# A fused attention kernel: instruction orders planned with TensorE's tile-mode turns counted once per turn, and jobs cut into single matmuls

## The chip, the core and the metric

One core of a Trainium2 chip runs the whole program in one launch. The metric is device time in microseconds, the median of several executions. Lower is better. The engines are TensorE (PE; its weight loads are PEld), VectorE (DVE), ScalarE (ACT), GpSimd (POOL) and SyncE (SP, which issues DMAs).

## The reference

Two attention blocks with their own inputs run side by side, each on 2,048 tokens of width 512 with 32 heads of 16. Their outputs are joined along the last axis.

```python
B, S, D = 1, 2048, 512
H = 32; Dh = D // H
# block A: linear attention
phi = lambda t: jnp.where(t > 0, t + 1, jnp.exp(t)) + 1e-6
pq, pk = phi(q), phi(k)
kv = jnp.einsum("bhsd,bhse->bhde", pk, v)
z = jnp.einsum("bhsd->bhd", pk)
num = jnp.einsum("bhqd,bhde->bhqe", pq, kv)
den = jnp.einsum("bhqd,bhd->bhq", pq, z)[..., None] + 1e-6
a = heads_joined(num / den) @ wo
# block B: softmax attention
scores = jnp.einsum("bhqd,bhkd->bhqk", q, k) * Dh ** -0.5
b = heads_joined(einsum("bhqk,bhkd->bhqd", softmax(scores), v)) @ wo
```

In both, q, k and v come from `x @ wqkv`. Most of the work is block B's exponential: 32 heads x 2,048 x 2,048 scores.

## The kernel before, in words

**Blocks.** The scores of block B are cut into 2,048 blocks of 128 keys by 512 queries, each for one head. They lie in 32 units. A unit is one group of eight heads (`Gp`, four of them), one stretch of 512 queries (`c`, four) and the even or odd heads of the group (`e_`, two), so a unit has 64 blocks: 16 stretches of keys for 4 heads. A score matmul (L709) contracts over 32 rows only, so that four of them, one for each 32-row quarter of TensorE's array, run side by side. It writes one block into one of seven PSUM banks.

**Two ways from scores to probabilities.** ScalarE takes two or three neighbouring banks in one exponential (L903, 1024 or 1536 columns wide). The banks of these pairs and triples are 0 and 1 with 2, and 4 and 5 with 3 (`SLOT`, `OPT`), used in turn. VectorE takes single blocks, or two at once where their banks are neighbours (L805), from the banks 6, 3 and 2 (`DSET`): it computes the bits of an approximate exponential as whole numbers. GpSimd makes two shifted copies of each such block with an integer addition (L977, mostly two blocks at once). The three versions are weighted by three scaled copies of v (L556) and summed, which makes the approximation finer. So a block of ScalarE costs one value matmul, and a block of VectorE costs three.

**Values.** A value matmul (L1031) has 17 output columns (16 of v and the sum) and sits in one quarter of the array's columns. Four of them, one for each head of the unit, run side by side: a round. They accumulate in one PSUM bank, `pPV`. At the end of a unit VectorE transposes that bank (L1051), takes reciprocals and normalizes (L1058, L1059).

**Jobs.** Projections, the linear block A and the output projections are cut into jobs: some matmuls into one of the banks of `DSET`, then VectorE or ScalarE work, and sometimes DMAs. L472, L547, L578, L604, L657 and others are their matmuls. Block A's phi needs 32 exponentials of 512 columns on ScalarE (L569).

**The planner.** The order on each engine is not written by hand. While the program is built, a list scheduler in Python (the loop at the end of the kernel function) keeps a planned clock `T` for each engine and a planned duration for each step. It repeatedly picks the step that can start first. What it can pick for TensorE: `fill_act_cand`, a pair or triple of scores for ScalarE, with up to two blocks for VectorE behind it (`d_pick`, `d_emit`); `fill_d_cand`, blocks for VectorE alone; `pv_cand`, a batch of value matmuls of up to `PVR` rounds; `job_cand`, the first matmuls of a job; and later pieces of jobs that run (`halves` cuts their matmuls into `parts`). Near the moment at which ScalarE would run out of scores (`dry`), only steps that end in time for the next pair may be picked. Planned idle time on TensorE of over about 0.2 us is filled with dummy matmuls on a zero weight (`fill_in`, L1237), which stand in the program as any other instruction. The result is one fixed order for each engine, with semaphores between them.

**Planned durations before.** A score group counts 0.33 us, a batch of values 0.1 + 0.215 for each round, a job matmul of 512 columns 0.26. TensorE works in three arrangements of its array: four quarters of rows for scores, four quarters of columns for values and dummies, the whole array for jobs. What a turn between them costs is contained in these numbers, whatever stands before a step.

Of the kernel before, what the change touches and what calls it, by code (L numbers as in the profile page):

```python
# [233 lines left out]
def bass_concat_heads__linear_attn_block__softmax_full_mha__prompt_kernel(nc, A_x, A_wqkv, A_wo, B_x, B_wqkv, B_wo, out):  # L234
# [3 lines left out]
    NGP = 4  # L238
# [19 lines left out]
    DLOW = 1.0  # L258
# [13 lines left out]
    with es:  # L272
# [132 lines left out]
        LAT = 0.12  # L405
        T = {"pe": 0.0, "act": 0.0, "dve": 0.0, "pool": 0.0, "dma": 0.0}
# [10 lines left out]
        class Job:  # L417
# [11 lines left out]
            def stage_done(self, i, end, bk, bi):  # L429
                if i == self.rel and bi is not None:  # L430
                    bfree[bi] = end + LAT
                    held[bi] = False
                for st, tk in self.gives:
                    if st == i:
                        tok[tk] = end + LAT
                if i + 1 < len(self.stages):
                    eng, dur, fn = self.stages[i + 1]
                    lat = LAT if eng != "pe" or eng != self.stages[i][0] else 0.0
                    push(eng, end + lat, JPR if eng == "pe" else (0 if i + 1 <= self.rel and self.bank else min(self.prio, 2)), dur,
                         lambda st_, en_, fn=fn: (fn(bk), self.stage_done(i + 1, en_, bk, bi)))  # L440
# [10 lines left out]
        MM = 0.26  # L451
# [50 lines left out]
        def gram_x(t4, **kw):  # L502
            def f(e, bk, i):
                tl, cc = divmod(i, 4)
                t = 4 * t4 + tl
                return e.matmul(f32v(bk)[:, tl * 128:(tl + 1) * 128], lhsT=xTb[:, cc, t * 128:(t + 1) * 128], rhs=xTb[:, cc, t * 128:(t + 1) * 128],
                                start=(cc == 0), stop=(cc == 3))
            return Job(halves(f, [("xTb", t) for t in range(4 * t4, 4 * t4 + 4)], n=16, parts=4, dur=0.07) + [
                        ("dve", 0.6, f_ev("dve", lambda e, bk: e.tensor_reduce(GRX[:, t4:t4 + 1], f32v(bk), axis=AX.X, op=ALU.max), [], [("GRX", t4)]))],
                       [("xTb", t) for t in range(4 * t4, 4 * t4 + 4)], [(4, ("GRX", t4))], **kw)  # L510

        def gram_w(kind, **kw):
            def f(e, bk, i):
                Gp, cc = divmod(i, 4)
                w = Wb[:, cc, kind * 512 + Gp * 128:kind * 512 + Gp * 128 + 128]
                return e.matmul(f32v(bk)[:, Gp * 128:(Gp + 1) * 128], lhsT=w, rhs=w, start=(cc == 0), stop=(cc == 3))
            gw = GRW[:, kind, :].rearrange("p (a h) -> p a h", h=8)
            return Job(halves(f, [("Wb", kind, g) for g in range(NGP)], n=16, parts=4, dur=0.07) + [
                        ("dve", 0.6, f_ev("dve", lambda e, bk: e.tensor_reduce(GRW[:, kind, :], f32v(bk).rearrange("p (h c) -> p h c", c=16), axis=AX.X,
                                                                                op=ALU.add, apply_absolute_value=True), [], [("GRW", kind)])),  # L520
                        ("dve", 0.15, f_op("dve", lambda e: e.tensor_tensor(gw, gw, ZMk[:].unsqueeze(1).broadcast_to([128, 4, 8]), op=ALU.mult),
                                           [("GRW", kind), "ZMk"], [("GRW", kind)])),
                        ("dve", 0.15, f_op("dve", lambda e: e.tensor_reduce(TOP[:, 1 + kind:2 + kind], GRW[:, kind, :], axis=AX.X, op=ALU.max),
                                           [("GRW", kind)], [("TOP", 1 + kind)]))],
                       [], [(6, ("TOP", 1 + kind))], rel=4, **kw)
# [17 lines left out]
        def v4_job(t4, Gp, **kw):  # L543
# [6 lines left out]
            st = halves(mm, [("Wb", 2)] + [("xTb", t) for t in ts], n=16, parts=2, dur=0.085)  # L550
# [24 lines left out]
        def akv_mm(t2, hp, kind):  # L575
            def mm(e, bk, i):
                tt, cc = divmod(i, 4)
                return e.matmul(f32v(bk)[:, 256 * tt:256 * tt + 256], lhsT=xTa[:, cc, (t2 + tt) * 128:(t2 + tt + 1) * 128],  # L578
                                rhs=Wa[:, cc, 512 * kind + 256 * hp:512 * kind + 256 * hp + 256], start=(cc == 0), stop=(cc == 3))
            return halves(mm, ["Wa", ("xTa", t2), ("xTa", t2 + 1)], n=8, parts=2, dur=0.14)  # L580
# [11 lines left out]
        def akvsum_job(hp, bl, **kw):  # L592
# [3 lines left out]
            st = halves(mm, [("KNa", t) for t in range(NT)] + [("VNa", t) for t in range(NT)] + ["VNa1"], n=16, parts=4, dur=0.1)  # L596
# [14 lines left out]
        def aden_job(sc, **kw):  # L611
# [5 lines left out]
            return Job(halves(f, [("PQT", 0, bq) for bq in range(4)] + [("RHZ", bq) for bq in range(4)], n=16, parts=4, dur=0.0625) + [  # L617
# [4 lines left out]
        def anum_job(sc, tl, **kw):  # L622
# [7 lines left out]
            return Job([("pe", 0.36, f_pe(f, [("PQT", 0, bq) for bq in range(4)] + [("RHA", bq) for bq in range(4)])),  # L630
# [206 lines left out]
        def fill_act_cand():  # L837
# [13 lines left out]
            if pt_room(2, start + 0.5) is None:  # L851
# [4 lines left out]
                start = later[0] - 0.5 + 1e-6  # L856
            def run(st, en):
# [37 lines left out]
                if tk:  # L895
                    d_emit(tk, en + 0.05)
                    T["pe"] = en + 0.05
# [12 lines left out]
            return start, 0.33, run  # L910

        def fill_d_cand():
# [15 lines left out]
            return at, 0.32, run  # L928
# [59 lines left out]
        def pv_cand():  # L988
# [13 lines left out]
            def batch(rd):  # L1002
                byg = [[x for x in rd if x[1][2] == g] for g in range(4)]
                best = None
                for rounds in range(1, PVR + 1):
                    bt = sum([q_[:rounds] for q_ in byg], [])
                    n = len(bt)
                    sc_ = n / (0.1 + 0.215 * rounds)
# [15 lines left out]
            dur = 0.1 + 0.215 * bb[1]  # L1024
# [166 lines left out]
        def job_cand():  # L1191
            best = None
            bi = d_bank()
            for lst, pr in ((urgent, 0.5), (early, 2), (bjobs, 2.2), (urgent2, 2.3), (ajobs, 2.5)):
                for pos, j_ in enumerate(lst[:1] if lst is not urgent2 else lst[:8]):
# [3 lines left out]
                    eng, dur, fn = j_.stages[0]  # L1199
# [5 lines left out]
                    if best is None or (st, pr) < (best[0], best[1]):  # L1205
                        def run(st_, en_, j_=j_, lst=lst, fn=fn):
# [6 lines left out]
                            j_.stage_done(0, en_, bk, b_)  # L1213
# [30 lines left out]
        while True:  # L1244
            opts = []
            for eng in T:
# [6 lines left out]
                if best is not None:  # L1253
                    c_ = best[2]
                    opts.append((best[1], c_[1], eng, c_[3], c_[4], c_))
            fa = fill_act_cand()
            if fa is not None:
                opts.append((fa[0], 0, "pe", fa[1], fa[2], None))
            fd = fill_d_cand()
            if fd is not None:  # L1260
                opts.append((fd[0], 3, "pe", fd[1], fd[2], None))
# [3 lines left out]
            if pc is not None:  # L1265
                opts.append((pc[0], pc[3], "pe", pc[1], pc[2], None))
            jc = job_cand()
            if jc is not None:
                opts.append((jc[0], jc[1], jc[2], jc[3], jc[4], None))
# [13 lines left out]
            st, _, eng, dur, run_, c_ = o  # L1283
# [96 lines left out]
```

## Time and profile before

| | |
|---|---|
| median of 3 runs | 740.53 us (740.44 to 741.14) |
| the profiled execution's own time | 741.09 us |
| its span, first to last instruction | 739.4 us |
| ScalarE busy | 711.2 us (96%) |
| TensorE busy by matmul records | 676.5 us (91%) |
| VectorE busy | 516.2 us (70%) |
| GpSimd busy | 327.2 us (44%) |
| blocks by ScalarE and by VectorE | 1,521 and 527 |

The page gives for each engine the time in which at least one of its instructions was running, and their number. A group's row has the line of code, the engine, the operation, what it writes and reads with the shape, the count, then busy time and the mean duration in ns of one, and behind the second bar the idle time of the engine just before, with what ended it. Durations of neighbours on one engine can overlap, so the pace of an engine is read from starts that follow each other. A row of the timeline has the start, the time from the first start to the last end, the engine, the line, the operation, and the count of merged instructions. The clock column says which share of full speed TensorE was granted; 1.00 is full.

### The profile page before, as it was taken

Reading aid. Unit: us, or ns where it says so; the run is one execution under the profiler, and the core shown is the slowest. Engines: PE = TensorE matmul, PEld = TensorE weight load, DVE = VectorE, ACT = ScalarE, POOL = GpSimd, SP = SyncE. Lnnn points to the kernel's source line nnn. Section 1 sums busy time; section 2 is a strip of 40 time slices with the busy share of each in tenths; the row PEclk is TensorE's granted clock in tenths of the full one; section 3 lists DMA queues with packets and bytes.
Section 4 is the critical chain, followed back from the end, with each engine's and each line's share of the span. In section 5 each row is a group of like instructions: output and inputs, shape, how many; then the busy total and the mean of one; then the engine's idle time right before and its main releaser. Section 6 shows DMA issues by size and latency. Waiting matters only on the chain.

```text
span 739.4 us, 15721 instructions
## 1 busy us (share of the span) xinstructions
PE 676.5 (91%) x6483; PEld 226.9 (31%) x6534; DVE 516.2 (70%) x865; ACT 711.2 (96%) x691; POOL 327.2 (44%) x562
## 2 busy tenths in 40 slices
PE   6999999999999999999899999889899999999996
PEld 4322333333333333233222223234222222222222
DVE  3887776765677667733688778845878777867771
ACT  3999999999999999999999999999999999999995
POOL 3455544522454434500356645500645475636560
PEclk9999999999999999999999999999999999999999
DMA  9900000000000000000201000000101100000001
GB/s 222 233 2 1 2 1 9 7 9 8 3 1 1 2 1 8 9 13 4 52 1 29 22 9 12 10 19 22 30 1 29 37 2 30 1 25 6 15 16 33
DMA packets 36573, 17.33 MB, mean 23 GB/s; under 512 B 27536, under 2 KB 35984, under 8 KB 36496
## 3 DMA queue, kind: packets, MB, share of 16 engines
q1 hardware_dynamic: 35408, 15.61, 8.8%
q8 instruction: 53, 0.87, 0.5%
q10 hardware_dynamic: 1088, 0.66, 0.3%
q14 instruction: 24, 0.20, 0.1%
HBM read 4.46 MB, written 4.19 MB: 12 GB/s over the span
## 4 chain that ended last, share of the span: by engine, by line
ACT 88%; PE 8%; issue 2%; DVE 1%; ACTq 0%; POOL 0%; POOLq 0%
ACT PT L903 86%; PE pS L709 3%; PE pPV L1031 2%; ACT EA L569 2%; PE pS L657 1%; PE pS L472 1%; PE pS L1120 0%; PE pS L1078 0%; DVE PT L805 0%; PE pPV L1237 0%; PE pS L1237 0%; ACT KNa L454 0%; PE pS L547 0%; PE pS L1109 0%; DVE KM L486 0%
## 5 line engine op out<-in xcount | busy, mean ns | idle before, releaser
L903 ACT ACTIVATE PT<-pS 128x1024 f16<-128x1024 f32 (+1 forms) x653 | 702.4, 1332 | 9.6 <-PE pS L709 9.4
L977 POOL INT64_ADD PT<-PT x537 | 319.8, 608 | 385.2 <-DVE PT L805 339.0
L805 DVE TENSOR_SCALAR PT<-pS 128x512 int16<-128x512 f32 (+1 forms) x503 | 339.5, 708 | 88.4 <-PE pS L709 84.0
L709 PE MATMUL pS<-QT,KM 32*128 32x512 bf16 x2048 | 281.8, 386 | 37.9 <-ACT PT L903 27.6
L1031 PE MATMUL pPV<-PT,VV 128*17 128x512 f16 x3102 | 269.8, 383 | 0.5 <-DVE OT L1051 0.4
L709 PEld LDWEIGHTS pS<-QT,KM 32*128 32x128 bf16 x2048 | 73.1, 91 | 280.6 <-ACT PT L903 228.7
L1031 PEld LDWEIGHTS pPV<-PT,VV 128*17 128x17 bf16 x3102 | 63.0, 88 | 122.7 <-issue 92.6
L1051 DVE STREAM_TRANSPOSE OT<-pPV 128x512 f32<-128x512 f32 x32 | 22.8, 713 | 30.5 <-PE pPV L1031 30.2
L578 PE MATMUL pS<-Wa,xTa 128*128 128x256 bf16 x256 | 38.7, 275 | 0.8 <-DVE PT L805 0.5
L472 PE MATMUL pS<-xTb,Wb 128*128 128x512 bf16 x98 | 29.8, 383 | 5.2 <-issue 2.1
L454 DVE CAST KNa<-pS 128x512 bf16<-128x512 f32 x30 | 20.5, 686 | 18.5 <-PE pS L657 17.0
L1237 PE MATMUL pPV<-xTb,ZW 128*17 128x256 bf16 x180 | 31.7, 274 | 0.0
L570 DVE TENSOR_SCALAR EA<-EA 128x512 bf16<-128x512 bf16 x32 | 11.7, 365 | 22.5 <-ACT EA L569 22.4
L569 ACT ACTIVATE EA<-pS 128x512 bf16<-128x512 f32 x32 | 26.1, 815 | 0.0
L578 PEld LDWEIGHTS pS<-Wa,xTa 128*128 128x128 bf16 x256 | 19.9, 97 | 17.9 <-issue 9.7
L547 PE MATMUL pS<-Wb,xTb 128*128 128x128 bf16 x256 | 19.5, 220 | 0.5
L1237 PEld LDWEIGHTS pPV<-xTb,ZW 128*17 128x17 bf16 x180 | 14.4, 91 | 15.0 <-issue 10.2
L657 PE MATMUL pS<-WOa,KNa 128*128 128x512 bf16 x52 | 15.6, 381 | 2.6 <-issue 1.4
L604 PE MATMUL pS<-xTa,Wa 128*128 128x512 bf16 x55 | 16.6, 383 | 1.3 <-issue 0.8
L482 DVE CAST QT<-pS 128x512 bf16<-128x512 f32 x15 | 10.3, 688 | 10.0 <-PE pS L472 9.8
L1059 DVE TENSOR_TENSOR OT<-OT,ZR 128x256 bf16<-128x256 f32 x32 | 16.6, 520 | 0.6
L547 PEld LDWEIGHTS pS<-Wb,xTb 128*128 128x128 bf16 x256 | 14.4, 98 | 8.0 <-issue 4.5
(78 smaller groups left out, 223.8 us busy)
## 6 DMA issues: line engine op xcount, KB each, us to landing
out_dram<-KNa SPq DMA_DIRECT2D x30, 128.0 KB, 1.7
Wa<-in_A_wqkv_dram SPq DMA_DIRECT2D x1, 1536.0 KB, 7.9
KM<-KR SPq DMA_DIRECT2D x96, 16.0 KB, 1.8
Wb<-in_B_wqkv_dram SPq DMA_DIRECT2D x2, 384.0 KB, 4.9
Wb<-in_B_wqkv_dram SPq DMA_DIRECT2D x1, 512.0 KB, 4.3
WOb<-in_B_wo_dram SPq DMA_DIRECT2D x1, 512.0 KB, 8.7
WOa<-in_A_wo_dram SPq DMA_DIRECT2D x1, 512.0 KB, 9.5
ON<-in_B_x_dram ACTq DMA_DIRECT2D x1, 256.0 KB, 2.7
```

Source lines behind the costliest of these rows:

```text
L472: return e.matmul(f32v(bk), lhsT=Wb[:, cc, kind * 512 + Gp * 128:kind * 512 + Gp * 128 + 128], rhs=xTb[:, cc, sc * 512:(sc + 1) * 512], st ...
L547: return e.matmul(f32v(bk)[:, tl * 128:(tl + 1) * 128], lhsT=xTb[:, cc, t * 128:(t + 1) * 128], rhs=Wb[:, cc, 1024 + Gp * 128:1024 + Gp * ...
L569: ("act", 0.06 + n * 0.000833, f_ev("act", lambda e, bk: e.activation(EA[:, q, 0:n], f32v(bk)[:, c0:c0 + n], ACTF.Exp), [], [("EA", q)])),
L578: return e.matmul(f32v(bk)[:, 256 * tt:256 * tt + 256], lhsT=xTa[:, cc, (t2 + tt) * 128:(t2 + tt + 1) * 128], rhs=Wa[:, cc, 512 * kind + 2 ...
L657: return e.matmul(f32v(bk), lhsT=src, rhs=WO[:, hb, :], start=(hb == 0), stop=(hb == 3))
L709: return e.matmul(dst, lhsT=KM[32 * g:32 * g + 32, Gp % 2, e_, j * 128:(j + 1) * 128], rhs=QT[32 * g:32 * g + 32, Gp % 2, c * 512:(c + 1) ...
L805: sch.add("dve", lambda e: e.tensor_scalar(PTi[:, i * 512:(i + n) * 512], PS[:, b0 * 512:(b0 + n) * 512], ESC, EB, op0=ALU.mult, op1=ALU.add),
L903: sch.add("act", lambda e: e.activation(PT[:, p0 * 512:p0 * 512 + w], PS[:, use[0] * 512:use[0] * 512 + w], ACTF.Exp, scale=SC), reads=[(" ...
L977: sch.add("pool", lambda e: e.int64_add(PTl[:, pos * 128:pos * 128 + w], PTl[:, p0 * 128:p0 * 128 + w], v_), reads=[("PT", p0 + i) for i i ...
L1031: sch.add("pe", lambda e, g=g, j=j, hl=hl, pi=pi, k=k, first=first, last_=last_: e.matmul(PVb[32 * g:32 * g + 17, 0:512], lhsT=VV[:, Gp % ...
L1051: sch.add("dve", lambda e: e.transpose(OT[:, 0, :], PVb[:, 0:512]), reads=[("PV", g) for g in range(4)], writes=[("OT", 0)])
L1237: ins = e.matmul(dst, lhsT=ZW[:, 0:17], rhs=xTb[:, 0, 0:256], start=first, stop=first, tile_position=(0, 32 * g))
```

## The change

The planner counts a turn of TensorE between scores (mode `q`) and anything else (mode `w`) as 0.1 us (`SW`), once, when the mode of the picked step differs from the one before. The steps themselves become shorter: a score group 0.222, a batch of values 0.2155 for each round + 0.005, a job matmul of 512 columns 0.226, and the narrower ones in proportion.

A job's part is no longer one piece. `halves` cuts each part into pieces of about 0.24 us, so single matmuls of 512 columns, two of 256, or four of 128. `Job.issue` and `Job.ran` hand them to the planner one after the other, and between two pieces it may pick a score group.

Batches of values have at most two rounds (`PVR` 2 instead of 3) and are taken from a lower yield on (`PVQ` 11 instead of 12.5). A new rule in `fill_act_cand` lets a score group wait, as long as ScalarE doesn't run dry, until two banks for VectorE's blocks are free (`WAITN`, `WAITM`), if VectorE has less than `DLOW` of work queued. `TEND`, by which jobs get the time from which they may start, is 670 instead of 640. No instruction of the kernel computes anything else than before; which blocks go to which engine, and the order, come out of the planner anew.

```diff
-    PVR = 3
-    PVQ = 12.5
-    PVO = 16
+    PVR = 2
+    PVQ = 11
+    PVO = 12
     RES = 8
+    WAITN = 2
+    WAITM = 0.05
...
-    TEND = 640.0
+    TEND = 670.0
...
-    DLOW = 1.0
+    DLOW = 1.5
...
+        SW = 0.1
+        mode = ["w"]
...
-        MM = 0.26
+        MM = 0.226
...
             w = n // parts
-            return [("pe", w * dur, mk(i * w, (i + 1) * w)) for i in range(parts)]
+            q = max(1, round(w * dur / 0.24))
+            while w % q:
+                q -= 1
+            v = w // q
+            return [("pe", w * dur, None, [(v * dur, mk(i * w + x * v, i * w + (x + 1) * v)) for x in range(q)]) for i in range(parts)]
...
+            if nfill[0] >= 2 and d_backlog(start) < DLOW and not lagging(start):
+                late = T["act"] + sum(exps) - 0.222 - SW - LAT - WAITM
+                now = sum(bfree[x] is not None and bfree[x] <= start + 0.05 for x in DSET)
+                if now < WAITN:
+                    t1 = sorted(bfree[x] for x in DSET if bfree[x] is not None and start + 0.05 < bfree[x] <= late)
+                    if t1:
+                        start = t1[0]
...
-            return start, 0.33, run
+            return start, 0.222, run
...
-            dur = 0.1 + 0.215 * bb[1]
+            dur = 0.2155 * bb[1] + 0.005
...
-                lim = max(dry - fa[1] - LAT - 0.05, fa[0])
-                keep = [o for o in opts if o[2] != "pe" or o[4] is fa[2] or o[0] + o[3] <= lim or o[0] + 1e-9 < fa[0] - o[3]]
+                lim = max(dry - fa[1] - SW - LAT - 0.05, fa[0])
+                keep = [o for o in opts if o[2] != "pe" or o[4] is fa[2] or o[0] + o[3] + (SW if mode[0] == "q" and o[6] == "w" else 0) <= lim]
...
             if eng == "pe":
                 fill_in(st)
+                if md != mode[0]:
+                    st = max(st, T["pe"] + SW)
+                    mode[0] = md
```

The added lines shift the numbers: L709 becomes L732, L805 L828, L903 L933, L977 L1007, L1031 L1061, L1237 L1268, L578 L601, L472 L495, L547 L570. What the planner makes of it in the program:

| in the built order | before | after |
|---|---|---|
| exponentials of 1024, 1536 and 512 columns (L903, L933) | 436, 216, 1 | 548, 116, 1 |
| VectorE's blocks, single and two at once (L805, L828) | 479, 24 | 497, 53 |
| GpSimd's additions for two blocks and for one (L977, L1007) | 517, 20 | 598, 10 |
| value matmuls (L1031, L1061) | 3,102 | 3,254 |
| rounds that they make | 889 | 944 |
| runs of score matmuls with nothing between | 632 | 666 |
| dummy matmuls (L1237, L1268) | 208 | 238 |

TensorE at the first job of block A, before (L709 scores, L1031 values, L578 the job):

```order
L709 MATMUL pS<-QT,KM 128x512 x4
L1031 MATMUL pPV<-PT,VV 17x512 x12
L709 MATMUL pS<-QT,KM 128x512 x3
L578 MATMUL pS<-Wa,xTa 128x256 x8
L709 MATMUL pS<-QT,KM 128x512 x3
L1031 MATMUL pPV<-PT,VV 17x512 x12
```

and after, at the same job:

```order
L732 MATMUL pS<-QT,KM 128x512 x3
L1061 MATMUL pPV<-PT,VV 17x512 x4
L601 MATMUL pS<-Wa,xTa 128x256 x2
L732 MATMUL pS<-QT,KM 128x512 x3
L601 MATMUL pS<-Wa,xTa 128x256 x4
L732 MATMUL pS<-QT,KM 128x512 x3
L601 MATMUL pS<-Wa,xTa 128x256 x2
L732 MATMUL pS<-QT,KM 128x512 x3
L1061 MATMUL pPV<-PT,VV 17x512 x8
```

The eight matmuls of the job stood in one piece. Now they are in three pieces with a score group between each two, and a batch of values has eight matmuls where it had twelve.

ScalarE from its first exponential on, before:

```order
L903 ACTIVATE PT<-pS 128x1536
L903 ACTIVATE PT<-pS 128x1024 x13
L903 ACTIVATE PT<-pS 128x1536
L903 ACTIVATE PT<-pS 128x1024
L903 ACTIVATE PT<-pS 128x1536
L903 ACTIVATE PT<-pS 128x1024 x3
L903 ACTIVATE PT<-pS 128x1536
```

and after:

```order
L933 ACTIVATE PT<-pS 128x1024 x21
L933 ACTIVATE PT<-pS 128x1536
L933 ACTIVATE PT<-pS 128x1024 x21
L933 ACTIVATE PT<-pS 128x1536 x5
L933 ACTIVATE PT<-pS 128x1024
```

Pairs take the place of triples: the bank that made a pair a triple (2 or 3) goes to a block for VectorE.

VectorE after its first reciprocals, before (L805 the blocks, L482 a job's copy):

```order
L805 TENSOR_SCALAR PT<-pS 128x1024
L805 TENSOR_SCALAR PT<-pS 128x512
L1059 TENSOR_TENSOR OT<-OT,ZR 128x16x16
L805 TENSOR_SCALAR PT<-pS 128x512 x5
L482 CAST QT<-pS 128x512
L805 TENSOR_SCALAR PT<-pS 128x512 x12
```

and after:

```order
L828 TENSOR_SCALAR PT<-pS 128x1024
L828 TENSOR_SCALAR PT<-pS 128x512 x4
L828 TENSOR_SCALAR PT<-pS 128x1024
L828 TENSOR_SCALAR PT<-pS 128x512 x4
L828 TENSOR_SCALAR PT<-pS 128x1024
L828 TENSOR_SCALAR PT<-pS 128x512 x4
```

More of its instructions take two blocks at once.

More of the change, by code (lines that the diff above doesn't have):

```diff
@@ L507, in f @@
                                 start=(cc == 0), stop=(cc == 3))
-            return Job(halves(f, [("xTb", t) for t in range(4 * t4, 4 * t4 + 4)], n=16, parts=4, dur=0.07) + [
+            return Job(halves(f, [("xTb", t) for t in range(4 * t4, 4 * t4 + 4)], n=16, parts=4, dur=0.058) + [
                         ("dve", 0.6, f_ev("dve", lambda e, bk: e.tensor_reduce(GRX[:, t4:t4 + 1], f32v(bk), axis=AX.X, op=ALU.max), [], [("GRX", t4)]))],
@@ L517, in gram_w @@
             gw = GRW[:, kind, :].rearrange("p (a h) -> p a h", h=8)
-            return Job(halves(f, [("Wb", kind, g) for g in range(NGP)], n=16, parts=4, dur=0.07) + [
+            return Job(halves(f, [("Wb", kind, g) for g in range(NGP)], n=16, parts=4, dur=0.058) + [
                         ("dve", 0.6, f_ev("dve", lambda e, bk: e.tensor_reduce(GRW[:, kind, :], f32v(bk).rearrange("p (h c) -> p h c", c=16), axis=AX.X,
```

53 lines of the change are left out of this document (33 added, 20 removed).

## The prediction

> **What bounds the kernel now.** I read the page first, then the chain, then the groups with their shapes kept apart, then the stretch between the first and the last exponential, and last single rows of the timeline, because a mean duration does not say how fast an engine accepts work.
>
> ```profile
> span 739.4 us, 15721 instructions
> PE 676.5 (91%) x6483; PEld 226.9 (31%) x6534; DVE 516.2 (70%) x865; ACT 711.2 (96%) x691; POOL 327.2 (44%) x562
> ...
> ACT 88%; PE 8%; issue 2%; DVE 1%; ACTq 0%; POOL 0%; POOLq 0%
> ACT PT L903 86%; PE pS L709 3%; PE pPV L1031 2%; ACT EA L569 2%; PE pS L657 1%; PE pS L472 1%; PE pS L1120 0%; PE pS L1078 0%; DVE PT L805 0%; PE pPV L1237 0%; PE pS L1237 0%; ACT KNa L454 0%; PE pS L547 0%; PE pS L1109 0%; DVE KM L486 0%
> ```
>
> ScalarE's exponentials (L903) are 86% of the chain. From here I call L709 a score matmul, L1031 a value matmul, L1237 a dummy, and the other TensorE work jobs. A block is one 128x512 score tile. The next row is the stretch from the start of the first exponential to the end of the last (14.69 and 729.53 us).
>
> ```profile
> 14.69:729.53 714.84, 663.80 (x6399) 218.41 (x6448) 509.50 (x847) 707.56 (x685) 321.59 (x544) 1.00 0.08 19
> ```
>
> The columns are PE, PEld, DVE, ACT, POOL, the clock, DMA. ScalarE is busy 707.56 of 714.84 us, so only 7.3 us of idle lie in the stretch. Outside it lie 14.7 us of start and 9.9 us of end. That gives the accounting that I use: 14.7 + 707.6 of ScalarE work + 7.3 idle + 9.9 = 739.5, against a span of 739.4, and 1.7 us around the span make this execution's 741.09. The median of the runs shown is 740.53, so 0.56 is taken off at the end.
>
> The groups show who shares the softmax blocks:
>
> ```profile
> L903 ACT ACTIVATE PT<-pS 128x1024 f16<-128x1024 f32 x436 | 441.8, 1187 | 6.7 <-PE pS L709 6.7
> L903 ACT ACTIVATE PT<-pS 128x1536 f16<-128x1536 f32 x216 | 326.5, 1627 | 2.9 <-PE pS L709 2.8
> L977 POOL INT64_ADD PT<-PT x537 | 319.8, 608 | 385.2 <-DVE PT L805 339.0 <-PE pS L709 34.1 <-issue 6.4
> L805 DVE TENSOR_SCALAR PT<-pS 128x512 int16<-128x512 f32 x479 | 310.9, 682 | 83.2 <-PE pS L709 79.2 <-issue 0.3
> ...
> L805 DVE TENSOR_SCALAR PT<-pS 128x1024 int16<-128x1024 f32 x24 | 29.3, 1220 | 5.2 <-PE pS L709 4.8
> ```
>
> Of the 2,048 blocks, ScalarE takes 436x2 + 216x3 and one more alone = 1,521. VectorE takes 479 + 24x2 = 527. The means of 1187 and 1627 ns are not what one exponential costs, because neighbours overlap. Their price is read from starts that follow each other without a gap:
>
> ```profile
> 67.87 0.89 ACT L569 ACTIVATE EA<-pS 128x512 bf16<-128x512 f32 x1
> 68.35 15.02 ACT L903 ACTIVATE PT<-pS 128x1024 f16<-128x1024 f32 x15
> 83.02 0.84 ACT L569 ACTIVATE EA<-pS 128x512 bf16<-128x512 f32 x1
> ...
> 324.24 0.85 ACT L569 ACTIVATE EA<-pS 128x512 bf16<-128x512 f32 x1
> 324.71 11.12 ACT L903 ACTIVATE PT<-pS 128x1536 f16<-128x1536 f32 x8
> 335.36 0.96 ACT L569 ACTIVATE EA<-pS 128x512 bf16<-128x512 f32 x1
> ```
>
> Eight wide ones take 335.36 - 324.71 = 10.65, or 1.331 us each. The fifteen from 68.35 to 83.02 stand in ScalarE's order as thirteen of 1024 and two of 1536: (14.67 - 2.66) / 13 = 0.924 us. An L569 takes 0.48 (67.87 to 68.35). The check is 436x0.924 + 216x1.331 + 33x0.48 (32 of L569 and the one exponential of 512) = 706.2, against 707.56 busy. So these prices carry the run.
>
> **The change, part by part.** The built order of the changed kernel has 548 exponentials of 1024, 116 of 1536 and one of 512, which is 1,445 blocks. VectorE has 497 + 53x2 = 603. So 76 blocks leave ScalarE. There are 112 more exponentials of 1024 (112x0.924 = 103.5) and 100 fewer of 1536 (133.1), so ScalarE has 29.6 us less to do. A second reading bounds it from above: (707.56 - 33x0.48) / 1,521 = 0.455 per block, times 76, is 34.6. From that goes the fixed part of twelve more instructions: 1.331 - 0.924 = 0.407 per block leaves 0.11 fixed, so 1.3, which makes 33.3. I take 29.6, the value from single rows, and keep 33.3 for the low end.
>
> The moved blocks cost the others. VectorE: 18x0.682 + 29x1.220 = 47.7, so 516 becomes 564 of about 711 us. GpSimd: 598 wide and 10 narrow additions instead of 517 and 20, so at most 81x0.608 = 49, and 327 becomes 376. Both stay well below ScalarE on the whole run. TensorE gets 152 more value matmuls (3,254 for 3,102, two extra for each moved block), more score groups and finer job pieces. Its slots, from the timeline:
>
> ```profile
> 299.70 0.83 PE L1031 MATMUL pPV<-PT,VV 128*17 128x512 f16 x12
> ...
> 300.46 0.40 PE L709 MATMUL pS<-QT,KM 32*128 32x512 bf16 x4
> ...
> 300.78 0.61 PE L1031 MATMUL pPV<-PT,VV 128*17 128x512 f16 x8
> ...
> 301.33 0.39 PE L709 MATMUL pS<-QT,KM 32*128 32x512 bf16 x3
> ```
>
> Twelve value matmuls, three rounds of four side by side, hold TensorE 0.76 us until the next score group, and eight hold it 0.55. So a round is 0.21 and 0.12 is the turn to scores. A score group with the turn away from it is 0.32 (300.46 to 300.78), so a group with both turns is 0.44. Job and dummy slots:
>
> ```profile
> 91.19 0.61 PE L578 MATMUL pS<-Wa,xTa 128*128 128x256 bf16 x4
> ...
> 91.73 0.39 PE L709 MATMUL pS<-QT,KM 32*128 32x512 bf16 x2
> ...
> 726.73 1.04 PE L1237 MATMUL pPV<-xTb,ZW 128*17 128x256 bf16 x8
> ```
>
> Four job matmuls of 256 columns take 0.54 - 0.12 = 0.42, or 0.41 ns a column. Eight dummies take 1.04 with a tail of about 0.27, or 0.11 each. Counted in the two orders: 632 runs of scores before, 666 now; 889 rounds of value matmuls (up to four column tiles each) before, 944 now; 208 dummies before, 238 now; about 297,000 job columns in both. The sum before is 632x0.44 + 889x0.21 + 122 + 208x0.11 = 278 + 187 + 122 + 23 = 610 us. After it is 293 + 198 + 122 + 26 = 639. Against a stretch of 714.84 the margin was 105 us. Against 714.84 - 29.6 = 685 it is 46. That margin hides the 29 us of added TensorE work, and without it they would cost up to 29 us.
>
> The page's own busy time says something else: 663.80 busy, and with 29 more it is 693, over the 685. By that reading TensorE paces the changed kernel. In the Trainium skill, Perfetto Trace Analysis, section Identifying the Most-Contended Engine, matmul busy time is called no good measure of how near TensorE is to its limit. This trace agrees that it is none, though here it reads high (663.8 against 610 of slots). By the rule the sum stays with the slots; by the busy time it would be the second rival's.
>
> The finer pieces bring 34 more score groups, each with a turn to scores and one away. A turn shows as 0.32 for a group that at 0.21 a round should take 0.21, so 0.11 to 0.12. Then 34x2x0.11 = 7.5 us, which stand within the 293. In the Trainium skill, TensorEngine Tiling (Array Packing), section Key Properties, a change of tiling mode is said to drain TensorE, which speaks against more changes. The rows agree that a turn costs, and set its size at 0.11.
>
> What remains is how much ScalarE waits. The waits of before:
>
> ```profile
> ACT PT L903 <- PE pS L709: 9.4, 12, 2.3
> PEld pS L709 <- ACT PT L903: 228.7, 544, 1.2
> ...
>   PEld pS L709: 15.4, 45
>   PEld pS L578: 4.9, 15
>   PEld pS L657: 3.9, 15
>   PEld pS L472: 3.2, 11
>   PEld pPV L1031: 3.1, 12
>   PEld pS L547: 2.0, 7
>   PEld pS L627: 1.3, 5
> ```
>
> The indented rows are those who waited for VectorE's blocks (L805). ScalarE waited for scores only 12 times, 0.78 us each. TensorE waited for a free score bank 544 times, so it mostly runs ahead. With the margin halved I expect about 4 more waits, 3 us. Below, none of the 7.3 is left. Above, the second rival. The new rule that holds a score group back until a second vector bank is free writes no wait of its own into the program. It only decides which score matmuls stand together, and the extra one waits behind the pair that ScalarE needs. Queued behind it on TensorE are value matmuls and then the next pair. Start and end stand alike in both orders, so 14.7 and 9.9 stay.
>
> The sum: 741.09 - 29.6 + 3.0 = 714.5 for an execution like the profiled one, and 714.5 - 0.56 = 713.9 beside the median: 714.
>
> **The rivals.** *The turns reach ScalarE.* If the 34 added groups fall where no margin is left, their 7.5 us come on top of 711.5 - 0.56 with the 3 us of waits: about 721. For it: job pieces of one or two matmuls now stand between pairs. Against it: 544 waits for a free bank. In the Trainium skill, TensorEngine Tiling (Array Packing), Key Properties, the drain at a change of mode is what would act here. Chance 0.10.
>
> *TensorE and VectorE pace together.* The seven rows of waits on VectorE are 33.8 us. Grown with its blocks (603/527) they are 39, and 639 + 39 = 678 of 685: no margin. If a third of the 39 reaches ScalarE, 711.5 + 13 = 724. For it: TensorE's queue is in order, so a vector score that waits holds the pair behind it. Against it: those waits are short, 0.34 us each in the first row (15.4/45). Chance 0.16.
>
> *Slower: scores that wait for a vector bank in front of a pair.* The price is 0.34 us a wait. The margin of 46 has to be used up and then the 29.6, so 76 us, which are about 220 more waits of this kind among 666 groups, every third. With 240 of them it is 746. VectorE at 79% speaks a little for it, the 45 such waits of before against it. Chance 0.03.
>
> *Waits vanish.* If ScalarE's idle of 7.3 goes almost wholly and the 33.3 holds, it is 741.09 - 33.3 - 2 - 0.56 = 705. Chance 0.07.
>
> *It changes nothing.* The blocks move, yet just as much idle appears on ScalarE, 29.6 us or about 38 more waits of 0.78. Chance 0.02.
>
> **How the numbers follow.** My forecast, between 707 and 719, keeps 0.62. All cases but two are faster: 0.95. A measurement of this kernel can tell about 0.2% from no change (1.5 us; its three runs span 740.44 to 741.14). Within that lies 0.02, slower 0.03. The range takes in most of the first two rivals and the low end of the gain: 705 to 728.
>
> **What would show it.** Right: about 1,445 blocks in the L903 successor with ScalarE busy about 678 us and idle between exponentials near 10; TensorE's waits for ScalarE's banks fewer than 544 and shorter in sum; VectorE near 564 busy, GpSimd near 370. Wrong: ScalarE idle before exponentials of 20 us or more, spread over many waits (the turns, if TensorE was running jobs; the second rival, if VectorE released it), or a start or end that grew. If the prices of an exponential differ from 0.924 and 1.331, the first term fails.

## The result, and the profile after

The changed kernel takes 718.81 us (median of 4 runs, 717.50 to 721.31) against 740.83 in the same measurement: a ratio of 0.9707, 95% interval 0.9679 to 0.9735. The forecast was 714, between 705 and 728. The profiled execution is the slowest of the four, 721.31 us with a span of 719.6, and it is the one that is read here. The top of its page and its chain:

```profile
span 719.6 us, 16347 instructions
PE 693.6 (96%) x6716; PEld 227.8 (32%) x6716; DVE 551.8 (77%) x912; ACT 686.8 (95%) x703; POOL 372.2 (52%) x633
...
PE 72%; ACT 21%; DVE 4%; issue 2%; POOL 0%; ACTq 0%; DVEq 0%; POOLq 0%
PE pPV L1061 26%; PE pS L732 24%; ACT PT L933 20%; PE pS L680 4%; PE pS L495 4%; PE pS L601 3%; DVE PT L828 2%; PE pPV L1268 2%; PE pS L570 2%; PE pS L627 2%; ACT EA L592 1%; DVE OT L1081 1%; PE pS L650 1%; PE pS L618 1%; PE pS L529 1%
```

ScalarE was 88% of the chain and is 21%. TensorE, 8% before, is 72%, spread over values, scores and jobs. ScalarE's busy share of 95% shows none of that. Next the groups with shapes apart, then the stretch from the first exponential to the end of the last (columns as before):

```profile
L933 ACT ACTIVATE PT<-pS 128x1024 f16<-128x1024 f32 x548 | 524.3, 1049 | 13.8 <-PE pS L732 10.7 <-DVE PT L828 0.5
L933 ACT ACTIVATE PT<-pS 128x1536 f16<-128x1536 f32 x116 | 167.4, 1491 | 0.5 <-PE pS L732 0.3
```

```profile
13.43:709.65 696.22, 681.80 (x6632) 219.66 (x6630) 545.69 (x895) 683.16 (x697) 367.61 (x617) 0.99 0.08 21
```

The stretch is 696.2 us instead of 714.8. ScalarE is busy 683.2 of it and idle 13.1, where it was busy 707.6 and idle 7.3. The start is 13.4 us (14.7 before) and the end 9.9 as before. The mean duration of an exponential of 1024 fell from 1187 to 1049 ns: they begin less far ahead of the end of the one before (half of all exponentials by 0.28 us or more before the change, by 0.13 after it). The waits between the two engines moved as well:

```profile
PEld pS L732 <- ACT PT L933: 149.0, 376, 1.2
...
PEld pS L732 <- DVE PT L828: 17.9, 47, 2.4
...
ACT PT L933 <- PE pS L732: 11.0, 17, 3.3
```

TensorE waits for a score bank of ScalarE 376 times instead of 544. ScalarE waits for scores 17 times instead of 12, and one wait is 3.3 us long. That one lies in the start, seen engine by engine: GpSimd, VectorE, ScalarE, then TensorE's clock in three stretches.

```profile
L1007 POOLq MODIFY_POOL_CONFIG  x2: 11/11/11, 16.6 to 16.6; - x2
```

```profile
22.86 1.20 POOL L1007 INT64_ADD PT<-PT  x2 [6.37 <-PE pS L732]
```

```profile
20.76 0.74 DVE L509 TENSOR_SCALAR KM<-pS,PAR 128x512 bf16<-128x512 f32 x1
24.16 1.29 DVE L828 TENSOR_SCALAR PT<-pS 128x512 int16<-128x512 f32 x2 [2.65 <-POOL PT L1007]
25.36 1.23 DVE L579 TENSOR_SCALAR VV<-VV 128x544 bf16<-128x544 bf16 x2
```

```profile
27.83 1.02 ACT L933 ACTIVATE PT<-pS 128x1024 f16<-128x1024 f32 x1 [3.30 <-PE pS L732]
29.40 1.02 ACT L933 ACTIVATE PT<-pS 128x1024 f16<-128x1024 f32 x1 [0.54 <-PE pS L732]
```

```profile
20.00:23.40 3.40, 3.38 (x43) 1.48 (x35) 1.50 (x3) 3.40 (x4) 0.55 (x1) 1.00 1.03 177
23.40:25.50 2.10, 0.00 (x0) 0.00 (x0) 1.34 (x3) 1.13 (x2) 2.10 (x5) 1.00 1.09 215
25.50:32.60 7.10, 6.97 (x40) 1.23 (x40) 5.82 (x10) 3.70 (x4) 4.59 (x9) 0.52 1.08 291
```

GpSimd's first addition starts at 22.86 us, 6.3 us behind its change of configuration at 16.6 (before: 23.11). In all fourteen traces of this case, those of the experiments below included, it comes 5.7 to 6.9 us behind the change of configuration, whatever the order asks for. The planner takes GpSimd as free from the start. The new order asks VectorE for more blocks early, and one of them waits 2.65 us for GpSimd. TensorE stands behind VectorE with no matmul from 23.4 to 25.5. Then the granted clock is 0.52 for 7 us, and ScalarE is busy only 3.7 of 7.1 us. In the Trainium skill, GPSIMD Engine Reference, section Instruction dispatch, the first call of a freshly loaded GpSimd kernel is said to cost about 6 us more, with no instruction of its own in the profile. The 6.3 us here agree.

### The profile page after: what moved, and what is told of

It reads as the page before. It is cut to its first block, busy times and chain, and to the rows that moved or that the text cites. A ratio compares the mean times of both kernels' runs of the same rounds, so it can differ in the third digit from the quotient of the medians.

```text
span 719.6 us, 16347 instructions
## 1 busy us (share of the span) xinstructions
PE 693.6 (96%) x6716; PEld 227.8 (32%) x6716; DVE 551.8 (77%) x912; ACT 686.8 (95%) x703; POOL 372.2 (52%) x633
## 4 chain that ended last, share of the span: by engine, by line
PE 72%; ACT 21%; DVE 4%; issue 2%; POOL 0%; ACTq 0%; DVEq 0%; POOLq 0%
PE pPV L1061 26%; PE pS L732 24%; ACT PT L933 20%; PE pS L680 4%; PE pS L495 4%; PE pS L601 3%; DVE PT L828 2%; PE pPV L1268 2%; PE pS L570 2%; PE pS L627 2%; ACT EA L592 1%; DVE OT L1081 1%; PE pS L650 1%; PE pS L618 1%; PE pS L529 1%
## 5 line engine op out<-in xcount | busy, mean ns | idle before, releaser
L933 ACT ACTIVATE PT<-pS 128x1024 f16<-128x1024 f32 (+1 forms) x665 | 672.4, 1126 | 14.3 <-PE pS L732 11.0
L1007 POOL INT64_ADD PT<-PT x608 | 364.8, 613 | 319.8 <-DVE PT L828 276.2
L828 DVE TENSOR_SCALAR PT<-pS 128x512 int16<-128x512 f32 (+1 forms) x550 | 380.8, 733 | 67.7 <-PE pS L732 61.4
L1061 PE MATMUL pPV<-PT,VV 128*17 128x512 f16 x3254 | 290.5, 385 | 2.8 <-DVE OT L1081 2.7
L732 PE MATMUL pS<-QT,KM 32*128 32x512 bf16 x2048 | 280.0, 386 | 8.1 <-ACT PT L933 3.7
L732 PEld LDWEIGHTS pS<-QT,KM 32*128 32x128 bf16 x2048 | 72.7, 91 | 238.5 <-ACT PT L933 149.0
L1061 PEld LDWEIGHTS pPV<-PT,VV 128*17 128x17 bf16 x3254 | 63.1, 88 | 127.4 <-issue 100.2
L601 PE MATMUL pS<-Wa,xTa 128*128 128x256 bf16 x256 | 41.3, 276 | 1.1 <-DVE PT L828 0.8
L1081 DVE STREAM_TRANSPOSE OT<-pPV 128x512 f32<-128x512 f32 x32 | 22.7, 710 | 23.4 <-PE pPV L1061 23.3
L495 PE MATMUL pS<-xTb,Wb 128*128 128x512 bf16 x120 | 38.2, 385 | 0.5 <-DVE PT L828 0.3
L1268 PE MATMUL pPV<-xTb,ZW 128*17 128x256 bf16 x206 | 34.7, 275 | 0.0
L601 PEld LDWEIGHTS pS<-Wa,xTa 128*128 128x128 bf16 x256 | 18.7, 97 | 22.8 <-issue 13.8
L680 PE MATMUL pS<-WOa,KNa 128*128 128x512 bf16 x64 | 20.9, 386 | 0.7 <-DVE PT L828 0.5
L570 PE MATMUL pS<-Wb,xTb 128*128 128x128 bf16 x256 | 20.9, 221 | 0.2 <-DVE PT L828 0.2
L1268 PEld LDWEIGHTS pPV<-xTb,ZW 128*17 128x17 bf16 x206 | 16.5, 91 | 14.1 <-issue 9.1
L627 PE MATMUL pS<-xTa,Wa 128*128 128x512 bf16 x64 | 19.9, 384 | 0.9 <-DVE PT L828 0.8
L592 ACT ACTIVATE EA<-pS 128x512 bf16<-128x512 f32 x32 | 20.1, 629 | 0.0
L570 PEld LDWEIGHTS pS<-Wb,xTb 128*128 128x128 bf16 x256 | 14.4, 98 | 10.4 <-issue 7.6
L680 PE MATMUL pS<-WOb,ON 128*128 128x512 bf16 x48 | 15.2, 385 | 0.0
```

The source lines that it names most:

```text
L495: return e.matmul(f32v(bk), lhsT=Wb[:, cc, kind * 512 + Gp * 128:kind * 512 + Gp * 128 + 128], rhs=xTb[:, cc, sc * 512:(sc + 1) * 512], st ...
L627: return e.matmul(f32v(bk), lhsT=Wa[:, cc, bq * 128:(bq + 1) * 128], rhs=xTa[:, cc, sc * 512:(sc + 1) * 512], start=(cc == 0), stop=(cc == 3))
L680: return e.matmul(f32v(bk), lhsT=src, rhs=WO[:, hb, :], start=(hb == 0), stop=(hb == 3))
L732: return e.matmul(dst, lhsT=KM[32 * g:32 * g + 32, Gp % 2, e_, j * 128:(j + 1) * 128], rhs=QT[32 * g:32 * g + 32, Gp % 2, c * 512:(c + 1) ...
L828: sch.add("dve", lambda e: e.tensor_scalar(PTi[:, i * 512:(i + n) * 512], PS[:, b0 * 512:(b0 + n) * 512], ESC, EB, op0=ALU.mult, op1=ALU.add),
L933: sch.add("act", lambda e: e.activation(PT[:, p0 * 512:p0 * 512 + w], PS[:, use[0] * 512:use[0] * 512 + w], ACTF.Exp, scale=SC), reads=[(" ...
```

## The experiments

The theory: the gain is the 76 blocks that left ScalarE, which the cheaper costs of TensorE's steps allow; what is lost against the forecast is the start, and TensorE, which has so little left that ScalarE often gets its scores at the last moment. Rivals: the finer order feeds ScalarE better; the turns cost; ScalarE paces the changed kernel as it did before. Each experiment on the planner plans the whole order anew, except the three that add or take away dummies. "Work" is ScalarE's by the prices of the prediction (0.924, 1.331, 0.48 us), with 33 short exponentials in every row (e1, e4 and e13 have 32, so their work is 0.5 us less). Busy and idle are those of the stretch of exponentials, in the profiled execution.

| kernel | blocks on VectorE | work | busy | idle | median us | ratio to before (95%) |
|---|---|---|---|---|---|---|
| before | 527 | 706.2 | 707.6 | 7.3 | 740.83 | 1 |
| after | 603 | 676.6 | 683.2 | 13.1 | 718.81 | 0.9707 (0.9679 to 0.9735) |
| e1_share | 524 | 703.5 | 715.6 | 15.6 | 754.86 | 1.0176 (1.0151 to 1.0201) |
| e6_cost | 599 | 676.4 | 682.4 | 9.4 | 717.13 | 0.9673 (0.9651 to 0.9695) |
| e2_whole | 594 | 679.4 | 684.0 | 6.0 | 715.95 | 0.9657 (0.9637 to 0.9678) |
| e4_pv3 | 613 | 673.0 | 679.8 | 8.2 | 715.07 | 0.9626 (0.9609 to 0.9644) |
| e3_nowait | 591 | 681.2 | 687.1 | 9.2 | 720.38 | 0.9714 (0.9697 to 0.9731) |
| e11_pv3_whole | 595 | 678.9 | 685.8 | 10.8 | 721.27 | 0.9721 (0.9705 to 0.9737) |
| e12_pv3_whole_nowait | 604 | 675.0 | 680.1 | 9.4 | 714.21 | 0.9628 (0.9612 to 0.9644) |
| e5_pool | 597 | 678.9 | 684.2 | 6.4 | 716.52 | 0.9665 (0.9644 to 0.9687) |
| e13_margin | 592 | 681.3 | 689.1 | 7.7 | 722.74 | 0.9744 (0.9727 to 0.9760) |
| e7_nodummy | 603 | 676.6 | 682.8 | 13.0 | 723.20 | 0.9750 (0.9719 to 0.9780) |
| e9_before_more | 527 | 706.2 | 710.9 | 8.5 | 745.83 | 1.0040 (1.0024 to 1.0056) |
| e10_after_more | 603 | 676.6 | 699.9 | 32.2 | 757.53 | 1.0197 (1.0178 to 1.0215) |

The ratios are each against runs of before on the same chip (its medians there 740.8 to 742.7), so kernels are compared by ratio; 0.001 is 0.74 us.

**TensorE's margin, before and after.** One dummy matmul in front of each batch of values, in both kernels:

```diff
             def run(st, en):
+                g0 = bt[0][1][2]
+                f0 = pv_iss[u][g0] == 0
+                sch.add("pe", lambda e: e.matmul(PVb[32 * g0:32 * g0 + 17, 0:256], lhsT=ZW[:, 0:17], rhs=xTb[:, 0, 0:256], start=f0, stop=f0, tile_position=(0, 32 * g0)),
+                        reads=["ZW", ("xTb", 0), ("xTb", 1)], writes=[("PV", g0)], accum=("pv", u, g0))
```

> The kernel before with one dummy matmul of 256 columns put in front of each of its 471 batches of values, the plan and all else unchanged: about 471x0.107 = 50 us more on TensorE. Theory (TensorE had a margin of about 105 us): at most 5 us slower, 741 to 746. Rival (TensorE already paces the kernel before): the 50 us show, 765 or more.

> The same in the changed kernel: one dummy of 256 columns in front of each of its 573 batches, about 573x0.107 = 61 us more on TensorE. Theory (a margin of about 46 us, of which part is used by waits already): 25 to 50 us slower, 744 to 769. Rival (ScalarE alone paces the changed kernel too): at most 8 us slower, up to 727.

Both times lie where the theory had them. What one dummy costs is read from the rows: first a batch of eight values and the next score group of the changed kernel, then the same with a dummy in front.

```profile
304.77 0.61 PE L1061 MATMUL pPV<-PT,VV 128*17 128x512 f16 x8
305.31 0.46 PE L732 MATMUL pS<-QT,KM 32*128 32x512 bf16 x4
```

```profile
318.45 0.28 PE L1058 MATMUL pPV<-xTb,ZW 128*17 128x256 bf16 x1
318.46 0.70 PE L1065 MATMUL pPV<-PT,VV 128*17 128x512 f16 x8
319.09 0.39 PE L732 MATMUL pS<-QT,KM 32*128 32x512 bf16 x4
```

From the first row to the score group it is 0.54 us without and 0.64 with the dummy, so a dummy adds 0.10, and not quite the 0.107 of the expectations: 47 us in e9 and 57 in e10. Before loses 0.4%, or 5.6 us by the spans, with 47 us more on TensorE. The changed kernel loses 36 us, by the ratios as by the spans, with 57 us more. First the stretch, the chain and ScalarE's waits of the kernel before with its dummies, then the same of the changed one:

```profile
15.26:734.61 719.35, 691.61 (x6868) 261.25 (x6919) 509.19 (x847) 710.90 (x685) 321.27 (x544) 1.00 0.08 19
```

```profile
ACT 60%; PE 32%; DVE 3%; issue 3%; DMA 1%; POOL 0%; ACTq 0%; DVEq 0%; POOLq 0%
```

```profile
ACT PT L903 <- PE pS L709: 9.6, 12, 2.3
```

```profile
14.06:746.24 732.18, 712.26 (x7150) 264.69 (x7203) 553.91 (x895) 699.94 (x697) 367.78 (x616) 1.00 0.08 19
```

```profile
PE 86%; ACT 5%; DVE 5%; issue 3%; POOL 0%; ACTq 0%; POOLq 0%; DVEq 0%
```

```profile
ACT PT L933 <- PE pS L732: 28.1, 80, 2.0
```

Before, ScalarE waits 12 times with and without the dummies. After, it waits 80 times instead of 17. So the changed kernel had about 57 - 36 = 21 us of TensorE left, and the kernel before at least 47 - 5.6 = 41. The 21 are rather too many, since e10 has 3.4 us at half clock and the changed kernel 10. This shows that TensorE now sets a good part of the pace, and refutes the rival that ScalarE alone does.

The same runs show something that the forecast missed. In e10 ScalarE runs the very instructions of the changed kernel, yet it is busy 699.9 instead of 683.2. A busy ScalarE is not one at its pace. Two neighbouring exponentials of the changed kernel, then the next alone:

```profile
488.38 1.94 ACT L933 ACTIVATE PT<-pS 128x1024 f16<-128x1024 f32 x2
```

```profile
490.32 1.02 ACT L933 ACTIVATE PT<-pS 128x1024 f16<-128x1024 f32 x1
```

The third starts just where the two end, and takes 1.02 us. In a backlog the next one starts 0.92 us after the last, ahead of its end. Each exponential that gets its scores only as the one before it ends loses those 0.1 us, and the profile books them as busy. In the Trainium skill, ScalarE: Activation LUTs, section What ACT_TABLE_LOAD costs, back-to-back activations are said to overlap by about 93 ns, and the 0.10 us here agree.

Counted over whole traces, the next exponential begins no more than 0.02 us ahead of the end of the one before, or after a pause, 12 times in the kernel before, 64 times in the changed one and 177 times in e10. At 0.1 us each that is 1.2, 6.4 and 17.7 us. Another 3, 41 and 136 times it begins less than 0.085 us ahead and loses a part. ScalarE's busy time exceeds its work by 1.4, 6.6 and 23.3 us.

**The share held at that of before.** `d_pick` refuses a block for VectorE above a share; all else as changed:

```diff
+            if dcount[0] > DSHARE * (sum(UB - x for x in left) + 8):   # DSHARE = 0.2573
+                return None
```

> The changed planner with everything it has, but VectorE may take no more than about 25.7% of the blocks: the built order has 315 exponentials of 1024, 298 of 1536 and 524 blocks on VectorE, as good as the 527 of before. At 0.924 and 1.331 us ScalarE has 315x0.924 + 298x1.331 + 15.8 = 703.5 us of work, 27 more than the changed kernel's 676.6. Theory (the gain is the blocks that left ScalarE): the gain goes, 732 to 742 us, at the lower end if ScalarE's waits also fall back to those of before. Rival (the gain is the finer order, which feeds ScalarE better): it stays near 720.

It takes 754.9, slower than forecast by either theory. ScalarE's work is back at 703.5. With the start of 13.9 us and the end of 10.0 in its trace that alone makes a span of 727, so no order with this share could stay near 720: the gain goes with the blocks, and the rival (the finer order by itself) falls. The other 13 us over the expected end are not settled by this run: its order also holds 617 dummies (208 before) and TensorE leads its chain with 74%, so it is no clean twin of the kernel before.

**The costs alone.** Everything undone but the turn, the durations and the margin before ScalarE runs dry:

```diff
-            return [("pe", w * dur, None, [(v * dur, mk(i * w + x * v, i * w + (x + 1) * v)) for x in range(q)]) for i in range(parts)]
+            return [("pe", w * dur, mk(i * w, (i + 1) * w)) for i in range(parts)]
...
-    PVR = 2
-    PVQ = 11
-    PVO = 12
+    PVR = 3
+    PVQ = 12.5
+    PVO = 16
...
-    TEND = 670.0
+    TEND = 640.0
...
-    DLOW = 1.5
+    DLOW = 1.0
...
-            if nfill[0] >= 2 and d_backlog(start) < DLOW and not lagging(start):
+            if False:
```

> Only the costs of the change: turns counted once, the shorter durations, and nothing else (whole parts of jobs, batches of up to three rounds, no wait for vector banks, the old times of jobs). The built order has 496 exponentials of 1024, 152 of 1536 and 599 blocks on VectorE: 676.4 us of ScalarE work, as much as the changed kernel. Theory (the costs move the blocks and the blocks set the time): 717 to 723 us. Rival (pieces, smaller batches and the wait keep ScalarE fed): 726 us or more, with more idle before exponentials than the changed kernel's 14 us.

717.1, as the theory had it. The costs carry the whole gain; the rest of the change adds nothing that shows here. The turn, the shorter durations and the margin stand in e6 together, so which of them lets the blocks move is not shown.

**Single rules undone.** e2 has only the first part of that diff (whole parts of jobs), e4 only the batches (`PVR`, `PVQ`, `PVO`), e3 only the last part (no wait), e11 whole parts and batches, e12 these two and no wait. `TEND` and `DLOW` stay as changed in all five.

> The changed kernel with a job's part in one piece again (halves as before); all else as changed. The built order has 518 exponentials of 1024, 139 of 1536 and 594 blocks on VectorE, so 679.4 us of ScalarE work, 2.8 more. Theory (the blocks set the time, the pieces only let ScalarE's pairs stand on time): 719 to 724 us. Rival (the pieces are what makes the share possible, since a whole part holds the next pair back): ScalarE waits before a pair rise by 10 us or more, 730 us or slower.

> The changed kernel with batches of values of up to three rounds again and the old yields (3, 12.5, 16). The built order has 560 exponentials of 1024, 105 of 1536 and 613 blocks on VectorE: 673.0 us of ScalarE work, 3.6 less than the changed kernel. Theory (blocks set the time, the size of a batch matters little): 714 to 720 us. Rival (three rounds, 0.64 us and two turns, hold a pair back where a pair of 0.92 us is being computed): 723 us or more.

> The changed kernel without the rule that lets a score group wait for two vector banks. The built order has 530 exponentials of 1024, 132 of 1536 and 591 blocks on VectorE: 681.2 us of ScalarE work, 4.6 more than the changed kernel. Theory (the blocks set the time; the waits come from TensorE's load): 717 to 723 us, the waits as in the changed kernel or a little fewer. Rival (the rule itself puts the pairs too late and makes the small waits): 8 us or more of the waits go, 712 to 716.

> The changed kernel with both undone that cost nothing alone: batches of up to three rounds, and jobs' parts whole. 516 exponentials of 1024, 140 of 1536, 595 blocks on VectorE: 678.9 us of ScalarE work. Theory: near the two single undoings, 713 to 718 us, with 10 to 16 us of ScalarE's waits. Rival (small pieces and small batches stand in for each other, and without both a pair is held back by 0.64 us of values or 0.43 of a job): 722 us or more.

> As the last one, and without the wait for two vector banks; so only the costs, the start times of jobs (670) and VectorE's low mark (1.5) are left of the change. 519 exponentials of 1024, 135 of 1536, 604 blocks on VectorE: 675.0 us of ScalarE work. Theory (the costs alone carry the gain): 711 to 718 us. Rival (the rest of the change carries a part of 5 us or more): 722 us or more.

Whole parts gave 716.0 and batches of three rounds 715.1, a little better than all rules together, and e2 better than either side of its expectation. e4 and e12 are faster than the changed kernel clear of their intervals (0.9626 and 0.9628 against 0.9707), e2 only just, and so beat both kernels. But the effects don't add: the two undone together (e11) give 721.3, between the 718 at most of the theory and the 722 at least of its rival, and taking the wait away as well brings 714.2. Each of these kernels has another order throughout, so a difference of 3 to 7 us can't be put down to the rule that was undone. The nine orders with the new costs and dummies as planned (after, e2 to e6, e11 to e13) lie between 0.9626 and 0.9744, with 591 to 613 blocks on VectorE. That pieces or small batches are needed for the gain is refuted by e6 and e12, which have neither; which of them helps stays open.

**The start.** Only the planner's knowledge of GpSimd:

```diff
-        T.update(pe=8.1, act=7.2, dve=9.6)
+        T.update(pe=8.1, act=7.2, dve=9.6, pool=18.0)
```

> The changed kernel whose planner is told that GpSimd is taken until 18.0 of its planned time (about 23 us of the trace, when the first addition starts in both traces). ScalarE's work is 678.9 us, 2.3 more. Theory (the 3.3 us hole before the exponential at 27.8 us, and TensorE at half clock from 25.7 to 32.6 us, come from a VectorE block that waits for GpSimd's late first addition): hole and half clock go, 4 to 7 us less there, 714 to 717 us in all. Rival (TensorE falls to half clock at the start whatever waits there): 719 to 722.

716.5, though ScalarE has 2.3 us more work. The same part of the program in its trace, three stretches of 4 us, has TensorE at full clock, and ScalarE busy 11.1 of 12 us:

```profile
20.00:24.00 4.00, 4.00 (x50) 1.70 (x47) 4.00 (x8) 4.00 (x6) 1.40 (x3) 1.00 1.04 165
24.00:28.00 4.00, 3.74 (x37) 1.14 (x37) 4.00 (x8) 3.97 (x6) 3.36 (x6) 1.00 1.23 227
28.00:32.00 4.00, 4.00 (x42) 1.74 (x41) 3.65 (x7) 3.15 (x4) 3.46 (x7) 1.00 0.93 286
```

The hole and the half clock are gone. The other traces bear the cause out. Six have TensorE at half clock from about 26 us on (the changed kernel, e1, e3, e6, e7 and e10), and in each of them VectorE, ScalarE or TensorE waits 1.4 us or more for GpSimd's first additions just before. e2, e4, e5, e9, e11 and the kernel before have no half clock there and no such wait over 0.5 us; two waits of 1.0 and 1.35 us (e12, e13) passed at full clock. By the ratios e5 is 3 us faster than the changed kernel, with intervals that just overlap, and its order is new throughout, so what the hole costs in all is not settled.

**The dummies.** The changed order with `fill_in` returning at once, so that all else stays in its place:

> The changed kernel's order without its 238 dummy matmuls; nothing else moves (548, 116, 603 as in the changed kernel). They hold TensorE about 238x0.11 = 26 us. Theory (TensorE has so little left that its dummies now stand in front of pairs): ScalarE's idle outside the start shrinks by 3 to 8 us, 711 to 716 us. Rival (the dummies stand where TensorE has nothing to do, and keep its clock up): no gain, and more stretches at half clock, 719 to 730 us.

723.2: the rival. Taking 26 us from TensorE gained nothing, and its clock fell to half in four stretches ahead of the end, 24 us in all (10 in the changed kernel). In the longest, ScalarE is busy 7.9 of 10.2 us:

```profile
26.60:30.00 3.40, 3.40 (x25) 0.55 (x22) 2.84 (x5) 1.86 (x2) 1.66 (x4) 0.50 1.07 209
64.10:67.50 3.40, 3.34 (x27) 0.57 (x31) 2.86 (x7) 2.40 (x3) 0.61 (x2) 0.50 0.00 0
405.50:415.70 10.20, 9.93 (x76) 2.12 (x73) 5.01 (x10) 7.90 (x7) 2.75 (x6) 0.50 0.01 3
705.80:712.70 6.90, 5.21 (x22) 1.49 (x24) 1.94 (x4) 3.75 (x4) 0.00 (x0) 0.51 0.00 0
```

So the run does not tell how much the dummies hold pairs back. It tells that they can't simply be left out: what that freed went to more time at half clock.

**More margin for each pair.** On e4, the pair is planned 0.09 us earlier:

```diff
-    WAITM = 0.05
+    WAITM = 0.14
...
-                lim = max(dry - fa[1] - SW - LAT - 0.05, fa[0])
+                lim = max(dry - fa[1] - SW - LAT - 0.14, fa[0])
```

> The kernel with batches of three rounds, whose planner puts each pair 0.09 us earlier ahead of the moment at which ScalarE runs dry (0.14 instead of 0.05 at both places), because an exponential starts 0.43 us after the first score matmul in the traces and 0.34 in the plan. 533 exponentials of 1024, 130 of 1536, 593 blocks on VectorE: 681.3 us of ScalarE work, 8.3 more than with 0.05. Theory (the many small waits come from TensorE's load, whatever the margin): waits fall by less than the work rises, 716 to 722 us. Rival (they come from pairs planned too late): 8 us or more of the waits go, 713 us or less.

722.7, a little above the theory's 716 to 722. Idle falls only from 8.2 to 7.7 while ScalarE's work rises by 8.3. In this order the earlier pairs leave less room for VectorE's blocks (592 instead of 613), and that costs more than the waits.

## Why the prediction was right, and where it was off

Profiled execution against profiled execution, the forecast was 714.5 and it is 721.3. (It is the slowest of four; by the medians it is 713.9 and 718.8.) The terms, forecast and measured: start 14.7 and 13.4; ScalarE's busy time 707.6 - 29.6 = 678.0 and 683.2; its idle 10.3 and 13.1; end 9.9 and 9.9. The 6.8 us between are -1.3 + 5.2 + 2.8, and the rest is rounding.

- **The blocks that leave ScalarE.** Right in mechanism: the order's counts hold, and e1 and e6 show that the time goes with them. The size of 29.6 was too large: 24.4 came. The step that failed is "these prices carry the run". 0.924 us is the price in a backlog, where it still held, and the changed kernel has less of a backlog. Busy over priced work is 1.4 us before, 6.6 after, 23.3 in e10.
- **More waits, 3 us.** 5.8 instead. Of the three microseconds over it, the one wait of 3.3 us at the start is more than all. The prediction took the start as unchanged because its first rows stand alike. It did not follow what the added early blocks meet on GpSimd.
- **TensorE's margin of 46 us hides its added work.** Half right. The time fell as forecast, but the chain went over to TensorE, and e10 finds about 21 us left. The prediction counted no half clock and no waits on VectorE into TensorE's slots. Those waits are the rows of who waited for VectorE's blocks (L828), without GpSimd's:

```profile
  PEld pS L732: 17.9, 47
  PEld pS L601: 6.6, 18
  PEld pS L495: 4.0, 12
  PE pS L732: 3.0, 4
  PEld pS L680: 2.6, 8
  PEld pS L627: 2.3, 7
  PEld pS L570: 1.6, 4
  PEld pS L650: 1.6, 5
  PE pS L601: 0.8, 3
```

They sum to 40 us (35 before, counted alike), close to the 39 that the second rival forecast. The 639 of slots and these 40 make 679, near the 696 - 21 = 675 that e10 gives for TensorE. That rival (TensorE and VectorE pace together, 724) is thus partly what happened, and it was in part luck that the time came out near the forecast: TensorE ended up nearly level with ScalarE and not above it.

- **The turns reach ScalarE (721).** Not tried by themselves. e2, without the finer pieces, is 3.7 us faster than the changed kernel by the ratios, but its order differs everywhere.
- **The two rivals that are not faster** fell with the result, and *waits vanish* too.
- VectorE at 551.8 and GpSimd at 372.2 against 564 and 370: VectorE came out 12 us lower than the sum. Its blocks (L828) added 41.3 us of busy time where the sum of mean durations gave 47.7, and the rest of its work fell by 5.7.

## What to carry to other kernels

When an engine is the bound and a planner or a hand moves work off it, forecast the gain by the pace in a backlog, then ask what is left of the backlog: as the next engine comes level, the bound engine loses its overlap between neighbours, and its busy share still reads 95%. The chain and the count of waits show the change of pace; the busy share does not. Adding a known load to the suspected engine, in both kernels, measures its margin directly. A re-planned order is a draw: nine settings of this planner lie within 1.2% of each other, and what single rules seemed to give did not add up, so a difference of that size says little of the setting.

## What the runs showed of the hardware

Ahead of the end, TensorE's granted clock fell to about half for 3.4, 6.8 or 10.2 us at a time in these traces (in the kernel before once, for 3.4 us at 629.9). In the changed kernel it did behind a stretch with no matmul of 2.1 us at the start, which e5 removed together with the half clock. But it also did at 411.4 us, where no such hole precedes:

```profile
404.00:408.00 4.00, 4.00 (x38) 1.35 (x37) 2.69 (x5) 4.00 (x5) 3.34 (x6) 1.00 0.00 0
408.00:411.40 3.40, 3.03 (x40) 1.21 (x37) 2.17 (x4) 3.40 (x4) 0.00 (x0) 1.00 0.01 2
411.40:414.90 3.50, 3.50 (x32) 0.55 (x29) 2.18 (x5) 2.27 (x3) 1.22 (x2) 0.51 0.01 2
```

Matmuls cover 3.03 of the 3.4 us ahead of it; among them are sixteen of block A's denominators (L638), only 8 columns wide. In e11 and e12 the clock also falls within 2 us of the end of sixteen of these (at 414.1 and 406.2 us). But each of the fourteen traces has four such groups, and no fall begins behind the other 53, so the narrow matmuls alone don't do it. What set the clock down was not tried and stays open. In the changed kernel it cost one wait of 1.2 us at 414.5.
